# Softmax sums of batches 4 to 7: from TensorE matmuls with a matrix of ones to VectorE sums over turned 32 by 32 squares

## The chip, the core and the metric

One core of a Trainium2 chip runs the whole kernel. The metric is the device time of one execution in microseconds (us). The engines are named as in the profile: PE (TensorE matmul) and PEld (its weight loads), DVE (VectorE), ACT (ScalarE), POOL (GpSimd) and SP (SyncE, used here only to issue transfers).

## What is computed

Attention with projected keys and values (8 batches, 8 heads, 1024 tokens, head size 64; keys and values are projected from 1024 rows down to 64), then a two-layer network with a hard-swish between, on 8192 tokens of width 512 and an inner width of 2048:

```python
k_proj = einsum('ks,bhsd->bhkd', E, k)          # 64 projected keys
v_proj = einsum('ks,bhsd->bhkd', F, v)
scores = (q @ k_proj^T) / sqrt(64)
attn   = exp(scores - max)                      # the kernel leaves the max out
attn   = attn / (sum(attn, axis=-1) + 1e-9)     # <- the softmax sums in question
x      = (attn @ v_proj), heads side by side    # 8192 x 512
h      = x @ w_in                               # 8192 x 2048
out    = (h * clip(h + 3, 0, 6) / 6) @ w_out    # 8192 x 512
```

For one batch the softmax sums are 8 heads x 1024 tokens: each adds 64 numbers.

## The kernel before, in words

A block `b` of the main loop (from line 632) runs the network of batch `b` and, woven into it, the attention of batch `b+1` (`second`) and the key and value projection of batch `b+2` (`third`). A block has two halves `t` of 512 tokens. A half has 16 first groups (`first_group`, line 512: 16 matmuls into one `mm` tile, then `h_out`: Relu by ACT into `r`, a multiply by DVE into `g`) and four slots in which a second group of the half before runs (`second_group`, line 521: 64 matmuls into one `mm` tile, which ACT copies to `o_sb` and SP sends out). From block 2 on the slots stand after first groups 3, 7, 11 and 15; numbered through a block they are slots 0 to 7. The table `plan` (lines 638 to 651) says at which quarter of which slot a piece of attention work is put in. The order on every engine's queue is the order in which the program text calls the instructions; no scheduler moves them.

For blocks 3 to 6 (attention of batches 4 to 7) the plan before is: slot 0, scores and exps of head pairs `j` = 1, 2 and 3 (`j = 0` was done in slot 6 of the block before); slot 1, `all_sums`; slot 3, the projection of batch `b+2`; slot 4, values and products of `j = 0, 1`; slot 6, values and products of `j = 2, 3`, and the scores of `j = 0` of the next batch. Small pieces are put off into the list `later`, one of which is popped after each first group.

`exps` (line 241) writes `aT[j]`, the exponentials: on partitions 64 `t` + key, 2 x 2 x 256 elements for parity `r`, head `a` of the pair and tokens. `all_sums` (line 269) makes all 16 rows of sums of a batch with eight matmuls against the 0/1 matrix `halves`, into one `mm` tile; ACT takes Ln, and after the next first group `spread` (line 282) lets ACT take Exp of its negative (so the inverse), SP writes 16 rows of 512 to DRAM (`rows`) and reads them back eight times, each time one head's row spread over 64 partitions, into the four `rec` tiles: four of these reads on SP's queue, four on POOL's. `scaled` (line 264) multiplies the values' tiles by `rec` on DVE and writes `xT`, the network's input of the next block.

Buffers that matter: four `mm` and four `at` tiles (lines 61, 62) are taken in turn by every matmul group, so a group waits until the reader of the tile four back is done. `rec` has four, `o_sb` four, `r` four, `aT` five buffers. `turn` (line 217) puts the transposes of the next keys (`kT`) and queries (`qT`) on SP's queue after slot 3, and POOL starts the loads of another batch when `qT` has landed.

Of the kernel before, what the change touches and what calls it, by code (L numbers as in the profile page):

```python
# [8 lines left out]
f32 = mybir.dt.float32  # L9
bf16 = mybir.dt.bfloat16  # L10
AF = mybir.ActivationFunctionType
ALU = mybir.AluOpType
# [3 lines left out]
def kernel(  # L16
# [11 lines left out]
    nc = tc.nc  # L28
    B, H, S, D = q.shape
    KP = E.shape[0]  # L30
# [3 lines left out]
    P = 128  # L34
    SO = S // P
    KO = d_model // P
    FO = d_ff // P
    TOK = 512
    NB = S // TOK
# [13 lines left out]
    dram = ctx.enter_context(tc.tile_pool(name="dram", bufs=2, space=bass.MemoryType.DRAM))  # L53
    kqv_pool = ctx.enter_context(tc.tile_pool(name="kqv", bufs=2))
    qT_pool = ctx.enter_context(tc.tile_pool(name="qT", bufs=2))
    att = ctx.enter_context(tc.tile_pool(name="att", bufs=2))
# [9 lines left out]
    def pmm():  # L66
        return ps_mm.tile([P, TOK], f32, tag="mm", name="mm")
# [5 lines left out]
    def g_tile():  # L73
        return gpool.tile([P, FO, TOK], bf16, tag="g", name="g")
# [10 lines left out]
    halves = consts.tile([P, 2, 2, NB, KP // 8], bf16, name="halves")  # L85
# [52 lines left out]
    for i in range(SB):  # L138
        c = slice(i * FO // SB, (i + 1) * FO // SB)
# [20 lines left out]
    def q_transposed(b):  # L160

        t = qT_pool.tile([P, KO, 2, TOK], bf16, tag="qT", name="qT")
        nc.sync.dma_start_transpose(t.rearrange("p j a (m n) -> p (j a m) n", n=P),
                                    kqv[b]["q"].rearrange("p h s d -> p (h s d)"))
        return t
# [11 lines left out]
    def rec_tile():  # L177
        return att.tile([P, 2, TOK], f32, tag="rec", name="rec", bufs=4)
# [14 lines left out]
    class Attention:  # L193
# [47 lines left out]
        def exps(self, j, tiles, when=lambda f: f()):  # L241
            self.aT[j] = aT = att.tile([P, 2, 2, HT], bf16, tag="aT", name="aT", bufs=KO + 1)
            for r in range(2):
                when(lambda r=r: nc.scalar.activation(aT[:, r].rearrange("p a n -> p (a n)"), tiles[r],  # L244
                                                      AF.Exp, scale=scale))


        def quads(self, stationary, j, allocs):
            tiles = [alloc() for alloc in allocs]
            for t in range(NB):  # L250
                for a in range(2):
                    r, c = t * KP, a * D
                    nc.tensor.matmul(tiles[t][c:c + D].rearrange("p (r n) -> p r n", r=2),  # L253
                                     stationary(r, 2 * j + a),
                                     self.aT[j][r:r + KP, :, a, :], start=True, stop=True)
            return tiles

        def sums(self, j, *allocs):
# [10 lines left out]
        def all_sums(self):  # L269
            den = pmm()  # L270
            for i in range(2):
                for c in range(4):
                    j, a = 2 * i + c // 2, c % 2
                    nc.tensor.matmul(den[32 * c:32 * c + 32].rearrange("p (r n) -> p r n", r=2),  # L274
                                     halves[:, i].rearrange("p i t n -> p (i t n)"), self.aT[j][:, :, a, :],
                                     start=(i == 0), stop=(i == 1))
            few = att.tile([P, TOK], f32, tag="few", name="few", bufs=1)
            nc.scalar.activation(few, den, AF.Ln)
            later.append(lambda: self.spread(few))


        def spread(self, few):
            nc.scalar.activation(few, few, AF.Exp, scale=-1.0)
            rows = dram.tile([H * NB, TOK], f32, tag="rows", name="rows")
            nc.sync.dma_start(out=rows, in_=few[::8])
            by_head = rows.rearrange("(c i t) n -> i c (t n)", c=4, t=NB)
            self.recs = [rec_tile() for _ in range(KO)]
            for h in range(H):
                (nc.sync, nc.gpsimd)[h % 2].dma_start(out=self.recs[h // 2][h % 2 * D:(h % 2 + 1) * D].rearrange("d t n -> d (t n)"),  # L289
                                  in_=by_head[h // 4, h % 4:h % 4 + 1].to_broadcast([D, NB * TOK]))  # L290

# [218 lines left out]
    def first_group(xT, t, g, fo):  # L512
        h_ps = pmm()
        h_part(h_ps, xT, t, fo, range(KO))
        h_out(h_ps, g, fo)
# [5 lines left out]
    def second_group(b, t, g, c, copy=None):  # L521
        o_dst = out_rows(b, t, c)
        if (b, t, c) == (B - 1, NB - 1, SB - 1):

            most = d_model * 3 // 4
            for piece, copy, dma in ((slice(0, most), nc.vector.tensor_copy, nc.sync),
                                     (slice(most, d_model), nc.scalar.copy, nc.scalar)):
                n = piece.stop - piece.start
                o_ps = pmm()[:, :n]
                for fo in range(FO):  # L530
                    in_columns(o_ps, g[:, fo, c * P:(c + 1) * P], w_out_sb[:, fo, piece],
                               start=(fo == 0), stop=(fo == FO - 1))
                o_sb = opool.tile([P, d_model], f32, tag="o_sb", name="o_sb")[:, :n]
                copy(o_sb, o_ps)  # L534
                dma.dma_start(out=o_dst[:, piece], in_=o_sb)
            return
        o_ps = pmm()
        for fo in range(FO):
            in_columns(o_ps, g[:, fo, c * P:(c + 1) * P], w_out_sb[:, fo, :],
                       start=(fo == 0), stop=(fo == FO - 1))  # L540
            if fo % SB == SB - 1:
                yield
        o_sb = opool.tile([P, d_model], f32, tag="o_sb", name="o_sb")
        (copy or nc.scalar.copy)(o_sb, o_ps)  # L544
        nc.sync.dma_start(out=o_dst, in_=o_sb)

    def whole(gen):
        for _ in gen:
            pass

    def x_tile():
        return xpool.tile([P, KO, NB, TOK], bf16, tag="xT", name="xT")
# [43 lines left out]
    second = Attention(1)  # L596
    second.xT = x_next

    def pop():
        if later:  # L600
            later.pop(0)()

    rows = [second_group(0, 0, g[0], c) for c in range(SB)]
# [27 lines left out]
    second = Attention(2)  # L631
    for b in range(1, B):
        if b + 1 < B:
            x_next = second.xT = x_tile()
        third = Attention(b + 2) if b + 2 < B else None


        plan = {}
        two = (pmm, pmm), (pat, pat)
        if b == 1:  # L640
            plan = {4: (4, second.all_scores), 5: (3, second.all_sums), 6: (2, second.first_values),
                    7: (2, lambda: second.some_values((2, 3), ((pmm, pmm), (pmm, pat))))}
        elif b + 1 < B:
            plan = {3 + (b == 2): (2, third.projected) if third else None,
                    4 + (b == 2): (2, lambda: second.some_values((0, 1), two)),
                    6: (2, lambda: second.some_values((2, 3), two, third))}
            if b == 2:
                plan.update({0: (2, second.projected), 1: (4, second.all_scores), 2: (4, second.all_sums)})
            else:
                plan.update({0: (1, lambda: second.some_scores((1, 2, 3), ((pmm, pmm), (pat, pat), (pat, pat)))),  # L650
                             1: (4, second.all_sums)})


        slots = (0, 4, 10, 15) if b == 1 else (3, 7, 11, 15)
        for t in range(NB):
            g = g_tile()
            for fo in range(FO):
                if b < 3 and t == 0 and fo < 2:

                    if fo == 0:  # L660
                        TwoGroups(xT, t, g).parts((0, 1, 2), (3,))
                else:
                    first_group(xT, t, g, fo)
                pop()
                if b == 1 and t == 0 and fo == 5:
                    second.projected()
                if not behind or fo not in slots:
                    continue
                n = t * SB + slots.index(fo)
                if (b, n) == (1, 7):  # L670
                    second.first_products()
                when, act = plan.get(n) or (None, None)

                rows = second_group(*behind[0], n % SB,
                                    nc.vector.tensor_copy if second and act == second.all_scores else None)
                for quarter in range(1, SB + 1):
                    next(rows) if quarter < SB else whole(rows)
                    if quarter == when:
                        act()
            behind = [(b, t, g)]  # L680
        if b == 1:
            later.append(lambda: qT_dma.update({3: q_transposed(3)}))
        second, xT = third, x_next
# [32 lines left out]
```

The softmax here doesn't subtract the row's maximum and nothing guards it: scores larger than these inputs give would overflow.

## Time and profile before

| what | value |
|---|---|
| median of 6 runs | 506.4 us (505.79 to 508.25) |
| the profiled execution: its time / its span | 505.89 us / 503.7 us |
| PE busy | 495.8 us, 98% of the span |
| DVE busy / ACT busy / POOL busy | 245.4 / 244.6 / 51.5 us |
| matmuls of `all_sums` (line 274), all batches | 48 in six groups, 379 ns each, several at a time |
| ACT's Ln and Exp of the sums (lines 278, 283) | 6 x 602 ns and 6 x 622 ns |
| DVE's multiply of a first group (line 510) | 256 x 687 ns |
| reads `rec<-rows`, issue to landing | 3.4 / 7.6 / 11.1 us (least, median, most) |
| writes `rows<-few`, issue to landing | 1.8 / 2.5 / 5.2 us |

The span is the time from the first to the last instruction in the profiler's record; the execution's own time has some 2.2 us more around it. A share of busy time is a mean over the whole span. "The chain that ended last" is followed back from the last instruction, at each step to what released it. Matmuls of 32 columns overlap: the duration of one says less than the time a run of them takes.

### The profile page before, as it was taken

To read this page: it belongs to the slowest core of one execution; us is meant where nothing else is said; L and a number is where in the kernel's file an instruction comes from. 1 tells how busy PE (TensorE), PEld (TensorE's weight loads), DVE (VectorE), ACT (ScalarE), POOL (GpSimd) and SP (SyncE) were. 2 spreads that over 40 slices of the span, in tenths; PEclk is the share of its full clock that TensorE was granted. 3 is DMA by queue.
4 is the path that set the end of the run, shared out by engine and by line. 5 is a ranking of instruction groups with operands and counts; after the bars stand their busy time and mean duration, and the time that the engine had idled before them with its cause. 6 is when DMAs were issued, how large, how long until landed. Compare 5 with 4: busy or idle time off the path is not lost.

```text
span 503.7 us, 18691 instructions
## 1 busy us (share of the span) xinstructions
PE 495.8 (98%) x8562; PEld 245.8 (49%) x8562; DVE 245.4 (49%) x384; ACT 244.6 (49%) x425; POOL 51.5 (10%) x82
## 2 busy tenths in 40 slices
PE   7999999999999999999999999999999999999997
PEld 3554554444454444444454444554444444444444
DVE  3572736834753573436633654446552365334420
ACT  3757476655355445533564344652456444343431
POOL 8620020021020120012001020010000100000000
PEclk9999999999999999999999999999999999999999
DMA  9999979689839989379933799156111711101112
GB/s 169 198 205 207 187 144 232 148 139 232 224 62 220 269 160 210 79 210 166 212 77 89 169 173 216 45 152 178 44 44 46 189 47 44 43 26 42 45 44 87
DMA packets 78815, 68.91 MB, mean 137 GB/s; under 512 B 36400, under 2 KB 67376, under 8 KB 78736
## 3 DMA queue, kind: packets, MB, share of 16 engines
q0 software_dynamic: 34400, 35.66, 42.4%
q1 hardware_dynamic: 44112, 31.73, 22.4%
q8 instruction: 67, 1.10, 0.9%
q10 hardware_dynamic: 224, 0.33, 0.2%
q14 instruction: 12, 0.10, 0.1%
HBM read 71.83 MB, written 16.97 MB: 176 GB/s over the span
## 4 chain that ended last, share of the span: by engine, by line
PE 92%; DMA 6%; POOL 1%; issue 1%; ACT 0%; DVE 0%; POOLq 0%; ACTq 0%
PE mm L175 85%; PE at L175 2%; DMA w_in_sb<-in_moe_w_in_dram 2%; DMA rec<-rows 2%; DMA k<-in_k_dram 1%; DMA rows<-few 1%; PE mm L253 1%; PE at L235 1%; PE mm L235 1%; PE at L253 1%; PE mm L274 1%; PE at L421 0%; POOL q L109 0%; POOL k L113 0%; POOL rec L289 0%
## 5 line engine op out<-in xcount | busy, mean ns | idle before, releaser
L510 DVE SCALAR_TENSOR_TENSOR g<-r,mm 128x512 bf16<-128x512 f32 x256 | 174.4, 687 | 190.0 <-ACT r L509 189.2
L175 PE MATMUL mm<-w_out_sb,g 128*32 128x512 bf16 (+3 forms) x3904 | 235.9, 376 | 0.0
L175 PE MATMUL mm<-xT,w_in_sb 128*32 128x512 bf16 (+1 forms) x3840 | 231.3, 379 | 0.6 <-DVE xT L266 0.4
L509 ACT ACTIVATE r<-mm 128x512 f32<-128x512 f32 x256 | 153.1, 600 | 71.4 <-PE mm L175 67.9
L175 PEld LDWEIGHTS <-w_in_sb 128*32 128x32 bf16 (+1 forms) x3840 | 110.3, 98 | 111.1 <-issue 1.7
L175 PEld LDWEIGHTS <-g 128*32 128x32 bf16 (+1 forms) x3904 | 109.3, 98 | 111.5 <-issue 6.7
L544 ACT COPY o_sb<-mm 128x512 f32<-128x512 f32 x57 | 33.4, 587 | 146.5 <-PE mm L175 141.5
L289 POOL DMA_DIRECT2D rec<-rows x24 | 12.6, 531 | 191.9 <-DVE g L510 131.4
L244 ACT ACTIVATE aT<-at 128x512 bf16<-128x512 f32 x38 | 21.2, 626 | 7.6 <-PE at L235 7.6
L266 DVE TENSOR_TENSOR xT<-at,rec 128x512 bf16<-128x512 f32 x31 | 19.8, 681 | 5.8 <-ACT rec L187 5.8
L266 DVE TENSOR_TENSOR xT<-mm,rec 128x512 bf16<-128x512 f32 x25 | 16.0, 685 | 5.2 <-PE mm L253 4.9
L211 DVE CAST kp<-at 64x512 bf16<-64x512 f32 x14 | 9.0, 678 | 11.6 <-PE at L175 11.6
L244 ACT ACTIVATE aT<-mm 128x512 bf16<-128x512 f32 x18 | 9.6, 598 | 10.3 <-PE mm L235 10.3
L175 PE MATMUL at<-k,e_t 128*32 128x512 bf16 (+1 forms) x104 | 13.3, 379 | 0.0
L175 PE MATMUL at<-v,f_t 128*32 128x512 bf16 (+1 forms) x104 | 13.2, 379 | 0.0
L225 POOL COPY mark<-qT 1x1 bf16<-1x1 bf16 x5 | 0.9, 177 | 118.7 <-DMA qT<-q 118.7
L214 DVE CAST vp<-at 64x512 bf16<-64x512 f32 x14 | 9.7, 694 | 0.4
L175 PEld LDWEIGHTS <-e_t 128*32 128x32 bf16 (+1 forms) x104 | 5.8, 98 | 5.9
L534 DVE COPY o_sb<-mm 128x384 f32<-128x384 f32 x1 | 0.6, 558 | 15.2 <-DMA out_dram<-o_sb 15.2
L235 PEld LDWEIGHTS <-kT 64*64 64x64 bf16 x224 | 5.7, 106 | 4.3 <-issue 3.3
L96 PE MATMUL mm<-ones 128*128 128x512 bf16 x18 | 6.3, 471 | 1.5 <-DVE halves L86 1.5
L544 DVE COPY o_sb<-mm 128x512 f32<-128x512 f32 x6 | 4.1, 686 | 6.0 <-PE mm L175 6.0
(70 smaller groups left out, 149.2 us busy)
## 6 DMA issues: line engine op xcount, KB each, us to landing
out_dram<-o_sb SPq DMA_DIRECT2D x63, 256.0 KB, 3.5
k<-in_k_dram POOLq DMA_DIRECT2D x7, 1024.0 KB, 11.3
v<-in_v_dram POOLq DMA_DIRECT2D x7, 1024.0 KB, 16.6
q<-in_q_dram POOLq DMA_DIRECT2D x7, 1024.0 KB, 20.4
rec<-rows SPq DMA_DIRECT2D x24, 256.0 KB, 7.4
rec<-rows POOLq DMA_DIRECT2D x24, 256.0 KB, 7.6
w_out_sb<-in_moe_w_out_dram POOLq DMA_DIRECT2D x4, 512.0 KB, 16.0
w_in_sb<-in_moe_w_in_dram POOLq DMA_DIRECT2D x5, 256.0 KB, 9.6
```

The costliest lines, as they stand in the source:

```text
L96: nc.tensor.matmul(ps, ones[:, :P], ones, start=True, stop=True)
L175: nc.tensor.matmul(ps[lo:lo + width[0]], stationary[:, lo:lo + width[0]], moving, **flags)
L211: nc.vector.tensor_copy(self.kp[:, :, a, :], self.ps[:KP].rearrange("p (h d) -> p h d", d=D))
L214: nc.vector.tensor_copy(self.vp[a * KP:(a + 1) * KP], self.ps[KP:].rearrange("p (h d) -> p h d", d=D))
L235: nc.tensor.matmul(tiles[r][t * KP:(t + 1) * KP, a * HT:(a + 1) * HT], self.kT[r * D:(r + 1) * D, 2 * j + a, :], qT[r * D:(r + 1) * D, j, ...
L244: when(lambda r=r: nc.scalar.activation(aT[:, r].rearrange("p a n -> p (a n)"), tiles[r], AF.Exp, scale=scale))
L253: nc.tensor.matmul(tiles[t][c:c + D].rearrange("p (r n) -> p r n", r=2), stationary(r, 2 * j + a), self.aT[j][r:r + KP, :, a, :], start=Tr ...
L266: when(lambda t=t: nc.vector.tensor_mul(self.xT[:, j, t, :], av[t], rec[:, t]))
L289: (nc.sync, nc.gpsimd)[h % 2].dma_start(out=self.recs[h // 2][h % 2 * D:(h % 2 + 1) * D].rearrange("d t n -> d (t n)"), in_=by_head[h // 4 ...
L509: nc.scalar.activation(r, h_ps, AF.Relu, bias=0.5, scale=1.0 / 6.0)
L510: nc.vector.scalar_tensor_tensor(g[:, fo, :], r, 1.0, h_ps, op0=ALU.min, op1=ALU.mult)
L544: (copy or nc.scalar.copy)(o_sb, o_ps)
```

## The change

The sums of batches 4 to 7 are made by DVE. `add_up(j)` sums `aT[j]` over squares of 32 partitions by 32 tokens that are turned on the way (`apply_transpose`), one instruction for each `j`: 128 x 1024 bf16 in, 128 x 32 f32 out. `spread_sums` turns the collected 128 x 128 sums again, adds the two halves of 32 keys (a copy to bring them to the same partitions, then an add, for each `t`), inverts 64 x 128 numbers, writes them to DRAM with two transfers in pieces of 32 numbers, and reads them back eight times, all on SP's queue. So that 32 neighbouring tokens lie beside each other, `exps` stores `aT` with head before parity, and the matmuls that read it (`quads`, `all_sums`) take 512 neighbouring elements. That layout holds for batches 1 to 7. Batches 2 and 3 keep `all_sums` and `spread`. In blocks 3 to 6 the plan becomes: slot 0, scores and exps as before, then `add_up(0)`; slot 1 at its half, `add_up(1, 2)`; slot 2 at its half, `add_up(3)` and `spread_sums`; slot 3, projection as before; slot 5 (before: 4), values and products of `j = 0, 1`; slot 6 as before.

```diff
         def exps(self, j, tiles, when=lambda f: f()):
             self.aT[j] = aT = att.tile([P, 2, 2, HT], bf16, tag="aT", name="aT", bufs=KO + 1)
             for r in range(2):
-                when(lambda r=r: nc.scalar.activation(aT[:, r].rearrange("p a n -> p (a n)"), tiles[r],
+                when(lambda r=r: nc.scalar.activation(aT[:, :, r, :], tiles[r].rearrange("p (a n) -> p a n", a=2),
                                                       AF.Exp, scale=scale))
+
+        def weights(self, j, a):
+            return self.aT[j][:, a].rearrange("p r n -> p (r n)")
...
-                    nc.tensor.matmul(tiles[t][c:c + D].rearrange("p (r n) -> p r n", r=2),
-                                     stationary(r, 2 * j + a),
-                                     self.aT[j][r:r + KP, :, a, :], start=True, stop=True)
+                    nc.tensor.matmul(tiles[t][c:c + D], stationary(r, 2 * j + a),
+                                     self.weights(j, a)[r:r + KP], start=True, stop=True)
...
+        def add_up(self, *js):
+            if 0 in js:
+                self.parts = att.tile([P, KO, 32], f32, tag="parts", name="parts", bufs=1)
+            for j in js:
+                nc.vector.tensor_reduce(out=self.parts[:, j], op=ALU.add, axis=mybir.AxisListType.X, apply_transpose=True,
+                                        in_=self.aT[j].rearrange("p a r n -> p (a r n)").rearrange(
+                                            "p (c i) -> p c i", i=32))
+
+        def spread_sums(self):
+            turned, other = [att.tile([P, KO * 32], f32, tag="turned", name="turned", bufs=2) for _ in range(2)]
+            inv = att.tile([KP, KO * 32], f32, tag="inv", name="inv", bufs=1)
+            nc.vector.transpose(turned, self.parts.rearrange("p j c -> p (j c)"))
+            for t in range(NB):
+                here, there = slice(t * KP, t * KP + 32), slice(t * KP + 32, (t + 1) * KP)
+                nc.vector.tensor_copy(other[here], turned[there])
+                nc.vector.tensor_add(inv[t * 32:(t + 1) * 32], turned[here], other[here])
+            nc.vector.reciprocal(inv, inv)
+            rows = dram.tile([NB, KO, 32, 32], f32, tag="turned_rows", name="turned_rows")
+            for t in range(NB):
+                nc.sync.dma_start(out=rows[t].rearrange("j c i -> c j i"),
+                                  in_=inv[t * 32:(t + 1) * 32].rearrange("c (j i) -> c j i", j=KO))
+            by_head = rows.rearrange("t j (a c) i -> j a t (c i)", a=2)
+            self.recs = [rec_tile() for _ in range(KO)]
+            for j in range(KO):
+                for a in range(2):
+                    nc.sync.dma_start(out=self.recs[j][a * D:(a + 1) * D],
+                                      in_=by_head[j, a:a + 1].to_broadcast([D, NB, TOK]))
...
         elif b + 1 < B:
-            plan = {3 + (b == 2): (2, third.projected) if third else None,
-                    4 + (b == 2): (2, lambda: second.some_values((0, 1), two)),
+            plan = {5: (2, lambda: second.some_values((0, 1), two)),
                     6: (2, lambda: second.some_values((2, 3), two, third))}
+            if third:
+                plan[4 if b == 2 else 3] = 2, third.projected
...
             else:
-                plan.update({0: (1, lambda: second.some_scores((1, 2, 3), ((pmm, pmm), (pat, pat), (pat, pat)))),
-                             1: (4, second.all_sums)})
+                def last_sums():
+                    second.add_up(3)
+                    second.spread_sums()
+
+                def three_scores():
+                    second.some_scores((1, 2, 3), ((pmm, pmm), (pat, pat), (pat, pat)))
+                    second.add_up(0)
+
+                plan.update({0: (1, three_scores), 1: (2, lambda: second.add_up(1, 2)), 2: (2, last_sums)})
```

## The prediction

> **What bounds the kernel now.** I read the page's busy table, then the chain that ended last in order of time, then the table of stretches, one per block, then the timelines of DVE and SP around the sums of batch 4 (block 3).
>
> ```profile
> PE 495.8 (98%) x8562; PEld 245.8 (49%) x8562; DVE 245.4 (49%) x384; ACT 244.6 (49%) x425; POOL 51.5 (10%) x82
> ```
> ```profile
> 198.66 9.61 PE mm L175 x176
> 208.27 0.43 PE mm L274 x8
> 208.71 12.09 PE mm L175 x224
> 220.79 1.73 PE at L175 x32
> 222.52 6.91 PE mm L175 x128
> 229.43 0.34 PE mm L253 x4
> ...
> 243.91 0.34 PE mm L253 x4
> 244.25 0.22 PE at L253 x4
> 244.47 0.22 PE at L235 x8
> ```
> ```profile
> 208.30:268.15 59.85, 59.85 (x1116) 29.29 (x1112) 29.54 (x44) 28.87 (x50) 4.96 (x8) 1.00 0.69 146
> ```
>
> The chain (start, length, what) is unbroken PE from 131 to 500 us. The stretch (length, then busy time of PE, PEld, DVE, ACT, POOL, then PE's granted clock) says so too: in a block of 59.85 us PE is busy for all of it at full clock, DVE and ACT for half. So a matmul taken out there is worth its place in the chain, and work given to DVE costs only what makes PE wait. PE runs 224 matmuls in 12.09 us, 54.0 ns each: a first group (16) is 0.86 us, a second group (64) 3.45 us. The eight of the sums take 0.43 us, the same rate.
>
> ```profile
> 205.50 0.69 DVE L510 SCALAR_TENSOR_TENSOR g<-r,mm 128x512 bf16<-128x512 f32 x1 [0.18 <-ACT r L509]
> 210.25 0.69 DVE L510 SCALAR_TENSOR_TENSOR g<-r,mm 128x512 bf16<-128x512 f32 x1 [4.06 <-ACT r L509]
> 211.26 1.41 DVE L510 SCALAR_TENSOR_TENSOR g<-r,mm 128x512 bf16<-128x512 f32 x2 [0.32 <-ACT r L509]
> 212.84 0.69 DVE L510 SCALAR_TENSOR_TENSOR g<-r,mm 128x512 bf16<-128x512 f32 x1 [0.17 <-ACT r L509]
> 217.16 0.69 DVE L510 SCALAR_TENSOR_TENSOR g<-r,mm 128x512 bf16<-128x512 f32 x1 [3.63 <-ACT r L509]
> ```
>
> DVE has a hole of some 4 us in every slot, while the second group runs (in brackets: its idle time). The new DVE work goes into these holes, behind the last multiply of the four first groups.
>
> **Removed from PE.** In each of four blocks 8 matmuls: 0.43 us each time, 1.73 us in all. Both neighbours have the same 128x32 form, so no gap goes or comes with them. ACT loses Ln and Exp, 1.22 us a block, off the path; one `mm` tile a block is no longer taken.
>
> **Added to DVE.** No row shows a turned sum, so I price it from rows with one input.
>
> ```profile
> L374 DVE CAST kp<-at 64x128 bf16<-64x128 f32 x8 | 1.9, 278 | 2.4 <-PE at L371 2.4
> L534 DVE COPY o_sb<-mm 128x384 f32<-128x384 f32 x1 | 0.6, 558 | 15.2 <-DMA out_dram<-o_sb 15.2
> L405 DVE COPY rec<-at 128x1024 bf16<-128x1024 bf16 x2 | 1.4, 683 | 0.0
> ```
>
> From 278 ns at 128 elements to 558 at 384 is 1.09 ns an element and 138 ns fixed: 1024 elements are 1.26 us. Least is the 683 ns of L405's 1024 elements; as most I take the element time twice, once to fill and once to empty the turned square: 2.38 us. I take 1.26. The rest of `spread_sums` is a turn, two copies and two adds of 128 elements, 0.28 us each by L374, and a reciprocal of 128 elements, 0.28 or, at eight times the elements' part, 1.26 us: 1.7 us, at most 2.7. A block gets 4 x 1.26 + 1.7 = 6.7 us, so DVE rises from 29.5 to 36 us of 59.4.
>
> Does it fit? Slot 0: `aT[0]` is old, DVE is free from 198.40 (last multiply at 197.71) to 202.91; even 2.38 fits. Slot 1: two sums from 206.19 end at 208.7. Without the sums' matmuls the first groups 8 to 11 run from 208.27 to 211.72. A multiply after a slot starts 1.54 us after the second group's end (215.62 to 217.16), so the next is due at 209.81. It fits with 1.1 us left. PE itself waits only if the multiply of group 8 isn't done (0.69) when slot 2's second group wants its `mm` tile at 211.72: the limit for one sum is (211.72 - 0.69 - 206.19) / 2 = 2.42 us. Slot 2: DVE is free 1.37 us after group 11 (220.44 - 219.07 for group 15), at 213.09; 1.26 + 1.7 end at 216.05, next due 216.72; PE waits from 217.94 on (slot 3's tile, 215.18 + 3.45 - 0.69). With both highest prices the end is 218.2, a wait of 0.2 us.
>
> The Trainium skill, page "VectorE: DVE Perf Modes", section "Rules for kernel authors", speaks against the change: of `tensor_reduce` on a hot path it says "Expect 1× — it's the slowest DVE op. Consider restructuring". Its section on the 1x mode makes the sum one element a cycle, an estimate of (1024 + 150) / 0.96 = 1.22 us, which fits the same hole; the page's warning would count only if DVE were the hot path, and the block's row says it is not.
>
> **Moved and added transfers.** The inverse is ready at 216.1 instead of 210.7. On SP there now stand two writes of 32 KB and eight reads; before, one write, four reads, and four on POOL.
>
> ```profile
> 210.76 0.51 SPq L285 DMA_DIRECT2D rows<-few  x1
> 213.69 2.75 SPq L289 DMA_DIRECT2D rec<-rows  x4
> 216.53 8.71 SPq L545 DMA_DIRECT2D out_dram<-o_sb  x2
> 225.41 1.25 SPq L218 DMA_TRANSPOSE kT<-kp  x1
> 226.71 4.29 SPq L163 DMA_TRANSPOSE qT<-q  x1
> ```
>
> Issues take 0.51 us each: the second write goes at 216.6, lands 2.5 (at most 5.2) us later, 219.1 to 221.8. Eight reads at 2.75 / 4 = 0.69 us are issued by 224.6 to 227.3, the four for `j = 0, 1` by 221.9 to 224.6; with 7.4 (at most 11.1) us to landing these are in by 229 to 236, the others by 232 to 238. Values now stand in slot 5: 229.43 - 0.43 + 6.91 = 235.9, products from 236.6. So the later slot pays for the later sums: 7 us of margin at the medians, none to speak of at the worst; `j = 2, 3` are wanted at 243.5 and have 6 us. A product that waited for `rec` would hold DVE's queue, hence the multiplies of slot 5's groups and, past some 1.7 us (0.5 free behind the four products, 1.2 of the `mm` tiles as in slot 1), PE.
>
> Behind the eight reads on SP wait the outputs of slots 2 and 3 (four `o_sb` buffers: not wanted for two slots), then `kT` and `qT`. The program reuses a DMA semaphore after eight transfers, so `qT` also waits for the fourth read to land, 229 to 236. With 6.1 us from issue to landing (8.3 at most in the trace) it comes at 235 to 244; the scores of the next batch want it at 244.0 (244.47 - 0.43). POOL's loads behind it started at 233.4 before, start 2 us later and have until 280. POOL loses four issues, 2.1 us a block.
>
> The Trainium skill, page "DMA: Bandwidth & Descriptors", section "Specifications", asks for pieces of at least 512 B; below, a transfer does a read-modify-write. The new write goes in pieces of 128 B, 256 of them, where the old one had 16 of 2 KB. No run here shows that price; 7 us more would still only use up the margin.
>
> **Layout.** `exps` writes two runs of 256 elements instead of 512, the matmuls read one run instead of two. L274 reads two runs at 54 ns like all others, so nothing is to be gained; for ACT the worst is two instructions of 256 (378 ns each in this trace) for one of 600, 0.9 us over the six in slot 0. ACT is idle 0.3 us behind them and the `mm` tiles give 1.2 us (211.72 - 0.69 - 209.81) more: nothing.
>
> **Sum.** -4 x 0.432 = -1.73 us. The profiled execution would go from 505.89 (span 503.7) to 504.16. It lies 0.5 us below the median of the runs, 506.4; the median would be 504.7, -0.34%. About 0.3%, 1.5 us, is what this kernel's measurement can tell from no change, so the whole gain lies just past that.
>
> **Rivals.**
> 1. The turned sum is slow, the one that ends slower. It decides from 2.42 us on (slot 1): each us more in one sum costs 2 us of PE there and, from about 3 us on, 1 us in slot 2. The gain of 0.43 is gone at 2.64 us. At four times the element time, 4.6 us, slot 1 loses 2 x (4.6 - 2.42) = 4.4 and slot 2 some 2.5: 27 us in four blocks, 531. For it: no turned sum in the trace. Against: no one-input row of DVE's above 1.1 ns an element.
> 2. The spread comes late (small pieces, one queue): `rec` past 238.3 or `qT` past 244.0 stalls PE by the same amount, four blocks (three for `qT`). 2 us late in each costs 6 to 8 us less 1.7: 510 to 513. For it: the worst landings use up the margin. Against: the medians leave 7 us.
> 3. Nothing measurable: part of the 1.73 is lost in small waits (a multiply late by tenths, other gaps at changes of matmul form, 0.12 us at the first values), 505.2 to 506.4. For it: the gain is thin. Against: PE has no idle time left for the loss to hide in.
>
> **How the numbers follow.** Forecast 0.67, rival 1 0.09, rival 2 0.08, rival 3 0.16. The forecast's own range is 503.8 to 505.4 (run noise of half a us; one less transition gap). The forecast falls short of 0.3% by noise in some 0.06 of cases, and rival 3 ends slower in 0.03: faster 0.61, same 0.19, slower 0.20. The range for 8 in 10 takes in rival 3 and its edge: 503.7 to 506.8.
>
> **What would show it.** Right: 32 fewer matmuls; block stretches of 59.4 us with PE busy throughout; `parts` near 1.26 us; products in slot 5 waiting for PE, not for a DMA; `mark` for `qT` near 235. Wrong: PE waiting for the multiplies into `g` in slots 2 or 3 (rival 1), for `xT` or `qT` in slots 5 or 6 (rival 2). What makes the prediction wrong is a turned sum above 2.4 us or a spread that takes over 20 us.

## The result, and the profile after

| | before | after |
|---|---|---|
| median | 506.53 us (505.64 to 508.88, 44 runs) | 503.75 us (503.07 to 507.24, 19 runs) |
| ratio, 95% interval | | 0.9946 [0.9936, 0.9956] |
| profiled execution / its span | 505.89 / 503.7 us | 503.87 / 502.1 us |
| PE / DVE / ACT / POOL busy | 495.8 / 245.4 / 244.6 / 51.5 us | 495.4 / 272.8 / 240.7 / 43.0 us |

The change makes the kernel faster by 2.7 us (0.54%); 1.73 us were forecast. PE's busy time falls by only 0.4 us in this pair, because in the first 20 us it is 1.0 us higher (17.25 against 16.22 us); what the change is worth is read from the blocks. First the chain that ended last in the kernel after (start, length, what), block 3 and the start of block 4:

```profile
199.08 21.70 PE mm L175 x400
220.78 1.73 PE at L175 x32
222.51 13.81 PE mm L175 x256
236.32 0.34 PE mm L256 x4
...
243.90 0.34 PE mm L256 x4
244.24 0.22 PE at L256 x4
244.45 0.22 PE at L235 x8
```

The piece `L274 x8` is gone and the 176 and 224 matmuls beside it have become one run of 400, still at 54 ns each. The values of `j = 0, 1` (now line 256) stand one slot later. From block 3 on there is no wait in it. The same stretch, from one projection to the next, in the kernel before and then in the kernel after (length, then busy time of PE, PEld, DVE, ACT, POOL with counts, granted clock, DMA share, GB/s):

```profile
220.79:280.65 59.86, 59.86 (x1117) 29.39 (x1112) 29.54 (x44) 28.86 (x50) 4.95 (x8) 1.00 0.72 151
```
```profile
220.78:280.21 59.43, 59.43 (x1109) 29.00 (x1104) 36.38 (x54) 27.93 (x48) 2.80 (x4) 1.00 0.73 147
```

Eight matmuls fewer, 0.43 us less, PE busy for all of both; DVE has 6.8 us more to do and nobody waits for it. The DVE timeline of the kernel after shows how near that is:

```profile
206.53 2.37 DVE L299 TRANSPOSE_TENSOR_REDUCE parts<-aT 128x32 f32<-128x1024 bf16 x2
210.24 0.69 DVE L543 SCALAR_TENSOR_TENSOR g<-r,mm 128x512 bf16<-128x512 f32 x1 [1.35 <-ACT r L542]
...
213.43 1.24 DVE L299 TRANSPOSE_TENSOR_REDUCE parts<-aT 128x32 f32<-128x1024 bf16 x1
...
216.17 0.94 DVE L313 RECIPROCAL inv<-inv 64x128 f32<-64x128 f32 x1
217.15 0.69 DVE L543 SCALAR_TENSOR_TENSOR g<-r,mm 128x512 bf16<-128x512 f32 x1
```

In slot 1 DVE is idle for 1.35 us behind the two sums. In slot 2 the reciprocal ends just as group 12's multiply is due (no brackets: no idle time before it). DVE's groups by form, for the prices (busy time, mean ns):

```profile
L299 DVE TRANSPOSE_TENSOR_REDUCE parts<-aT 128x32 f32<-128x1024 bf16 x16 | 19.4, 1229 | 0.0
L313 DVE RECIPROCAL inv<-inv 64x128 f32<-64x128 f32 x4 | 3.8, 945 | 0.1
L312 DVE TENSOR_TENSOR inv<-turned 32x128 f32<-32x128 f32 x8 | 2.2, 280 | 0.3
L311 DVE COPY turned<-turned 32x128 f32<-32x128 f32 x8 | 1.8, 219 | 0.2
L308 DVE STREAM_TRANSPOSE turned<-parts 128x128 f32<-128x128 f32 x4 | 1.2, 312 | 0.1
```

So four blocks account for 1.73 us of the 2.7. The last microsecond is not in the blocks. The end of the program: the last run of matmuls and the DMA table of the stretch behind it, before and then after:

```profile
422.32 77.88 PE mm L175 x1504
q8 instruction: 1, 0.02, 1.5%
issues: line engine op xcount, KB each, median us to landing
out_dram<-o_sb SPq DMA_DIRECT2D x1, 192.0 KB, 2.5
out_dram<-o_sb ACTq DMA_DIRECT2D x1, 64.0 KB, 2.1
```
```profile
421.02 77.88 PE mm L175 x1504
issues: line engine op xcount, KB each, median us to landing
out_dram<-o_sb SPq DMA_DIRECT2D x1, 192.0 KB, 1.9
out_dram<-o_sb ACTq DMA_DIRECT2D x1, 64.0 KB, 1.6
```

Before, one load on the instruction queue (`q8`, 16 KB) falls among the last two output transfers and both land later; after, there is none there. From PE's last matmul (500.20 and 498.90) to the end of the span it is 3.5 us before and 3.2 us after. And the time outside the span is 1.79 us in the mean of 19 runs, where the kernel before has 2.12 (29 runs). These two, the end and the time outside, were the open question for the experiments.

### The profile page after: what moved, and what is told of

The parts are those of the page before. It is cut to its first block, busy times and chain, and to the rows that moved or that the text cites. A ratio compares the mean times of both kernels' runs of the same rounds, so it can differ in the third digit from the quotient of the medians.

```text
span 502.1 us, 18625 instructions
## 1 busy us (share of the span) xinstructions
PE 495.4 (99%) x8530; PEld 245.7 (49%) x8530; DVE 272.8 (54%) x424; ACT 240.7 (48%) x417; POOL 43.0 (9%) x66
## 4 chain that ended last, share of the span: by engine, by line
PE 93%; DMA 4%; POOL 1%; issue 1%; ACT 1%; DVE 0%; POOLq 0%; ACTq 0%
PE mm L175 86%; PE at L175 2%; DMA rec<-rows 2%; DMA k<-in_k_dram 1%; DMA rows<-few 1%; PE mm L256 1%; PE at L235 1%; PE mm L235 1%; PE at L256 1%; PE at L454 1%; PE at L420 0%; POOL q L109 0%; PE at L434 0%; PE mm L454 0%; POOL k L113 0%
## 5 line engine op out<-in xcount | busy, mean ns | idle before, releaser
L299 DVE TRANSPOSE_TENSOR_REDUCE parts<-aT 128x32 f32<-128x1024 bf16 x16 | 19.4, 1229 | 0.0
L96 PE MATMUL mm<-ones 128*128 128x512 bf16 x18 | 7.4, 549 | 1.5 <-DVE halves L86 1.5
## 6 DMA issues: line engine op xcount, KB each, us to landing
v<-in_v_dram POOLq DMA_DIRECT2D x7, 1024.0 KB, 16.4
```

Source lines behind the costliest of these rows:

```text
L96: nc.tensor.matmul(ps, ones[:, :P], ones, start=True, stop=True)
L299: nc.vector.tensor_reduce(out=self.parts[:, j], op=ALU.add, axis=mybir.AxisListType.X, apply_transpose=True, in_=self.aT[j].rearrange("p a ...
```

## The experiments

**Is it POOL's queue?** One run gives POOL half of the reads back, the other takes them away from the kernel before.

```diff
-                    nc.sync.dma_start(out=self.recs[j][a * D:(a + 1) * D],
+                    (nc.sync, nc.gpsimd)[a].dma_start(out=self.recs[j][a * D:(a + 1) * D],
```

> The changed kernel with every second of the eight reads of a batch on POOL's queue again, as before the change. The chain of PE in blocks 3 to 6 stays as it is (59.43 us a block). Theory A (the part of the gain beyond the 1.73 us of the removed matmuls, about 1.0 us, comes from the 16 reads that left POOL's queue, at the end of the program and outside the span): the time goes back by 0.7 to 1.0 us, to a ratio near 0.9965, and the time outside the span rises from 1.77 to about 2.2 us. Rival B (the queue has nothing to do with it): ratio stays near 0.9946, 1.77 us outside the span.

Measured: 503.55 us, ratio 0.9943 [0.9925, 0.9962], 1.78 us outside the span, 59.43 us a block. Theory A falls: 16 reads more on POOL cost nothing.

```diff
-                (nc.sync, nc.gpsimd)[h % 2].dma_start(...
+                (nc.sync, nc.gpsimd)[h % 2 if self.b < 4 else 0].dma_start(...
```

> The kernel before, with all eight reads of batches 4 to 7 on SP's queue, POOL's none. PE's blocks stay at 59.86 us unless a product waits for its reads (slot 4 wants them some 16 us after the write). Theory A: faster by 0.7 to 1.0 us (ratio near 0.998), time outside the span 1.8 us in place of 2.2. Rival B: ratio 1.000 within 0.0007.

Measured: 506.56 us, ratio 0.9998 [0.9986, 1.0010]. That is rival B for the whole time. Yet the time outside the span did fall to 1.80 us, though in the run before it stayed at 1.78 with POOL's reads back. So the reads on POOL don't set it either.

**Do the matmuls carry the gain?** The eight matmuls run again in blocks 3 to 6; nobody reads their result, the sums still come from DVE.

```diff
+                def idle_sums():
+                    den = pmm()
+                    for i in range(2):
+                        for c in range(4):
+                            nc.tensor.matmul(den[32 * c:32 * c + 32], halves[:, i].rearrange("p i t n -> p (i t n)"),
+                                             second.weights(2 * i + c // 2, c % 2), start=(i == 0), stop=(i == 1))
...
+                def two_sums():
+                    second.add_up(1, 2)
+                    later.append(idle_sums)
...
```

> The changed kernel with the eight matmuls against the 0/1 matrix run again in blocks 3 to 6, their result unread. Theory of the forecast (PE's removed matmuls are 0.432 us a block): block stretches of 59.86 us and 1.73 us more than the changed kernel, a ratio near 0.998. Rival (the gain comes from elsewhere, the matmuls fill places that were free): within 0.3 us of the changed kernel, ratio 0.9946 to 0.9955.

Measured: 506.28 us, ratio 1.0005 [0.9987, 1.0022]. Its chain and its stretch from projection to projection:

```profile
198.41 10.47 PE mm L175 x192
208.89 0.43 PE mm L696 x8
209.32 11.22 PE mm L175 x208
```
```profile
220.54:280.40 59.86, 59.86 (x1117) 29.36 (x1112) 36.41 (x54) 27.95 (x48) 2.81 (x4) 1.00 0.75 146
```

DVE does the whole new work (36.4 us), and the block is back at 59.86. So the matmuls' place in PE's order is the gain of the blocks and the DVE work is free: the theory is right. But it predicted a return of 1.73 us, and by the medians 2.5 came back (the ratio's interval is 0.9 us to either side). The kernel's DMA table at the end shows the load again:

```profile
q8 instruction: 1, 0.02, 1.7%
issues: line engine op xcount, KB each, median us to landing
out_dram<-o_sb SPq DMA_DIRECT2D x1, 192.0 KB, 2.9
out_dram<-o_sb ACTq DMA_DIRECT2D x1, 64.0 KB, 2.4
```

**Is it the layout?** The kernel before with the new order of `aT` alone (`exps` and the operands of `quads` and `all_sums` as in the diff of the change).

```diff
-                when(lambda r=r: nc.scalar.activation(aT[:, r].rearrange("p a n -> p (a n)"), tiles[r],
+                when(lambda r=r: nc.scalar.activation(aT[:, :, r, :], tiles[r].rearrange("p (a n) -> p a n", a=2),
```

> The kernel before with only the new layout of the exponentials (two runs of 256 written, one run of 512 read by the matmuls). Forecast: nothing, ratio 1.000 within 0.0007, values' matmuls 0.34 + 0.22 us as before, ACT's exps within 0.03 us of 0.60 to 0.63. Rival C (the layout brings the rest of the gain): faster by about 1 us, ratio 0.998.

Measured: 506.54 us, ratio 1.0000 [0.9988, 1.0011]. ACT's exps take 598 and 629 ns in the mean, as before (598 and 626). Rival C falls; the layout is worth nothing, as forecast.

**Is it where the instruction loads fall?** PE's list before is 2 x 8562 instructions and the page counts 67 loads of together 1.10 MB: one load of 16 KB for 256 instructions, that is for 128 pairs of weight load and matmul, 6.9 us at 54 ns. In the trace of the kernel before the ten loads from 432.4 to 494.4 us stand 6.9 us apart. The removed sums are 64 instructions, a quarter of a period. Four runs shift the phase by small pairs (28 ns each) in place of warm-up matmuls at the start:

```diff
-    busy(12)
+    busy(8)
+
+    ps = pmm()
+    for _ in range(36):
+        nc.tensor.matmul(ps[:32, :32], ones[:, :32], ones[:, :32], start=True, stop=True)
```

The second has `busy(4)` and 72, the third and the fourth `busy(1)` and 107.

> The changed kernel with 32 small pairs of weight load and matmul more on PE, put at the start in place of four of the warm-up matmuls: PE's instruction list is as long as before the change (64 more), the work of the main loop is the changed kernel's. Theory P (phase: the instruction queue loads 16 KB, 256 of PE's instructions, every 6.9 us, and with 64 instructions more one load falls on the last two output transfers, as it does before the change and not after it): 0.6 to 1.0 us above the changed kernel, near 504.5 (ratio 0.9963), landing of the last transfers 2.5 and 2.1 us in place of 1.9 and 1.6, block stretches still 59.43 us. Rival Q (the list's length has nothing to do with it, the removed matmuls simply are worth more than 1.73 us): within 0.3 us of 503.7.

> As the run before with 64 small pairs (128 instructions more). Theory P: the load at the end comes 1.7 us earlier again, at about the last matmul's end, and touches the output transfers less: between 503.7 and 504.5. Rival Q: 503.7.

> As the run before with 96 small pairs (192 instructions more). Theory P: the load falls 1.9 us before the last matmul's end and is over before the last transfers; the time is the changed kernel's again, 503.7 within 0.3. A third theory L (a longer list costs in itself) would give more than with 32 or 64 pairs, above 504.5.

> The kernel before with 96 small pairs at the start in place of eleven warm-up matmuls: its list is 192 instructions longer, 256 more than the changed kernel's, so the loads fall as in the changed kernel. Theory P: 0.6 to 1.0 us faster than the kernel before (ratio 0.998 to 0.9988) with no work taken out. Rival Q: ratio 1.000; theory L: slower.

| run | median, us | ratio to before | last landings, us | end of PE to end of span, us |
|---|---|---|---|---|
| after + 64 instructions | 504.56 (6 runs) | 0.9953 [0.9939, 0.9967] | 2.9, 2.5 | 4.1 |
| after + 128 | 504.38 (5) | 0.9943 [0.9929, 0.9956] | 2.2, 1.7 | 3.3 |
| after + 192 | 504.65 (6) | 0.9955 [0.9941, 0.9969] | 1.9, 1.6 | 3.2 |
| before + 192 | 506.32 (12) | 0.9987 [0.9975, 1.0000] | 1.9, 1.6 | 2.9 |

The kernel before stood at 506.90 in these runs. Where the loads fall, theory P is right in all four: the load comes back to the end with 64 instructions more and leaves it with 192, in the kernel before too. The profiles (all but the one at half rate, further below) sort by the last load's start against the end of PE's last matmul:

- from 0.0 to 0.3 us behind it (before, the reads on SP, the matmuls put back, the layout, 64 instructions more): landings of 2.5 to 3.0 us and 2.1 to 2.5, a tail of 3.5 to 4.1 us, mean 3.8;
- some 0.5 us ahead of it (128 more): 2.2 and 1.7 us, a tail of 3.3;
- over 2 us ahead (after, the reads on POOL, the two with 192 more, and three of the runs below): 1.9 and 1.6 us, a tail of 2.9 to 3.2, mean 3.1.

Between the first and the last that is 0.7 us. In the medians the size isn't shown. By the ratios the first run is 0.35 us above the changed kernel and the fourth 0.65 us below the kernel before: theory P's way, the first by less than its 0.6 us. But the third, which should have been the changed kernel's again, is 0.45 us above it, and the intervals overlap. At 504.65 us it even meets theory L (above 504.5); the fourth, faster with the longest list of all, speaks against L. The exchanged warm-up work changes the start as well, which these runs don't separate: block 3's projection begins at 221.25, 221.34, 220.43 and 224.19 us in the four profiles, at 220.78 in the changed kernel's and 220.79 in that of the kernel before.

**How much room has DVE?** The two sums of slot 1 made three times over.

```diff
-... 1: (2, lambda: second.add_up(1, 2)), ...
+... 1: (2, lambda: second.add_up(1, 2, 1, 2, 1, 2)), ...
```

> The changed kernel with the two sums of slot 1 made three times over (six instead of two; the same values are written again). By the limit of the prediction's slot 1 (PE waits when the multiply of group 8 is not done as slot 2's second group starts, 4.85 us of DVE's work in that hole): six sums at 1.19 us are 7.1 us, so PE waits some 2.3 to 2.6 us in slot 2 of each of four blocks, block stretches of 61.9 us, 513 to 514 us. Rival (the `mm` tiles give less or more room than reckoned): no wait at all (503.8), or one of over 4 us a block (above 520).

Measured once: 511.78 us. Its chain, and what PE waited for (us in total, times, longest):

```profile
206.27 6.79 DVE parts L299 x6
213.06 0.58 DVE g L543
213.64 0.04 issue
213.68 8.82 PE mm L175 x160
```
```profile
PE mm L175 <- DVE g L543: 7.5, 4, 1.9
```

The six sums enter the chain, and PE waits 1.9 us in each block for a multiply into `g`. Six sums take 6.87 us on DVE's timeline, so the room is 6.87 - 1.9 = 5.0 us against 4.85 reckoned. The limit is there, and it is the one of the prediction. The time is below the 513 to 514 us expected: in a row of six a sum took 1.14 us, not 1.19, and the room is 0.15 us larger.

**Was the later slot needed?** Values of `j = 0, 1` back in slot 4.

```diff
-            plan = {5: (2, lambda: second.some_values((0, 1), two)),
+            plan = {(5 if b == 2 else 4): (2, lambda: second.some_values((0, 1), two)),
```

> The changed kernel with the values of j = 0, 1 back in slot 4 of blocks 3 to 6. Theory (the later slot pays for the later sums): the products would want `rec` at 229.8 in block 3's frame, the first four reads are issued by 222.2 and land 6.6 us (at most 10.6) later, 228.8 to 232.8: DVE waits for the reads there, 0 to 3 us, and PE for 0 to 1.5 us a block: 503.8 to 510. Rival (the reads are in time for slot 4 also, the move is worth nothing): products wait for PE only, 503.7.

Measured: 503.76 us, ratio 0.9946 [0.9930, 0.9961], which is the changed kernel's. DVE's timeline there:

```profile
229.03 0.70 DVE L214 CAST vp<-at 64x512 bf16<-64x512 f32 x1
229.76 1.29 DVE L268 TENSOR_TENSOR xT<-mm,rec 128x512 bf16<-128x512 f32 x2
230.96 1.28 DVE L268 TENSOR_TENSOR xT<-at,rec 128x512 bf16<-128x512 f32 x2
```

The products follow at once and don't wait for the reads. My theory falls: the move of the values is worth nothing at these landings.

**Can it go further?** Batch 3's sums (block 2) on DVE too, its reads on POOL.

```diff
-                plan.update({0: (2, second.projected), 1: (4, second.all_scores), 2: (4, second.all_sums)})
+                plan.update({0: (2, second.projected), 1: (4, second.all_scores),
+                             2: (1, lambda: second.add_up(0, 3, 1)), 3: (1, batch_3_sums)})
...
```

> The changed kernel with batch 3's sums (block 2) on DVE too: three sums in slot 2, the fourth and the spreading in slot 3, its eight reads on POOL's queue so that the transposes on SP's are not held up. Forecast: eight matmuls less, 0.43 us, 503.3 (ratio 0.9938) if the reads land before slot 5's products (first four issued by 229, in by 236, wanted at 236.7 in block 3's frame). Rival (the spread is late, block 2 has the loads of another batch beside it): PE waits 1 to 4 us in slot 5, 504 to 508.

> The kernel that also makes batch 3's sums on DVE, looked at once more, since the profiled execution before ran its matmuls at half rate from the first to the last (117 ns each) and tells nothing of the timed ones (510 to 515 us at granted clocks of 0.990 to 0.993). Theory: PE stalls 2 to 4 us in slots 5 or 6 of block 2, waiting for `xT` (late `rec`) or for the transposes, and after the stall the granted clock is halved for two or three stretches of 3.4 us, which cost 1.7 us each. Rival: no stall in block 2; the time is lost elsewhere (slots 2 and 3, DVE late with the multiplies).

Measured in the first: 1047.89 us in the profiled execution, 512.28 us in the median of the other five, ratio 1.0119 [1.0091, 1.0147]. In the second: 512.45 us, one execution. The forecast of 503.3 fails, and its rival's 504 to 508 is passed too. What PE waited for in the second, the chain there, and its stretches around the wait:

```profile
PE at L235 <- DMA qT<-q: 7.2, 1, 7.2
```
```profile
173.09 17.96 DMA qT<-q
191.04 0.04 issue
191.08 0.64 PE at L235 x6
191.73 15.47 PE mm L175 x240
```
```profile
182.00:185.40 3.40, 1.91 (x36) 0.57 (x24) 2.11 (x4) 0.27 (x1) 0.00 (x0) 1.00 1.14 105
185.40:188.80 3.40, 0.00 (x0) 0.10 (x1) 0.69 (x2) 0.00 (x0) 0.00 (x0) 0.64 1.33 121
188.80:192.20 3.40, 1.12 (x16) 0.47 (x19) 0.60 (x2) 0.43 (x1) 0.69 (x2) 0.50 0.84 222
192.20:195.60 3.40, 3.40 (x40) 1.29 (x36) 0.00 (x0) 0.94 (x3) 2.15 (x3) 0.50 0.61 77
195.60:199.00 3.40, 3.40 (x60) 1.48 (x56) 1.30 (x2) 1.87 (x4) 0.00 (x0) 0.86 1.12 149
```

The spread, one slot later, lies on top of the transposes: its reads were issued from 169.37 to 174.19, `qT` at 173.09. `qT` took 18 us to land (median in the changed kernel 9.6), and slot 6's scores waited 7.2 us for it. That the reads beside it made `qT` late is argued from this overlap; no run separates it from the loads of another batch. DVE waited for reads too (3.1 us in slot 6). Meanwhile the granted clock (third figure from the end) falls to 0.5 and is full again only from 199 on: the next 240 matmuls took 15.5 us in place of 13.1, 2.4 us more. 7.2 + 2.4 is more than twenty times the 0.43 us to be gained. The expectation of the second run named both the wait and the lower clock; the wait is longer than its 2 to 4 us. No version tried here beats the changed kernel.

## Why the prediction was right, and where it fell short

- *The range*: 503.75 us lies at the very edge of the 503.7 to 506.8 forecast, and just below the narrower 503.8 to 505.4. The mechanism forecast was right; that the time still fell within the wide range is partly luck, since another microsecond came from two terms that the sum didn't have (below).
- *Removed from PE, 1.73 us*: 0.43 us in each of four blocks, shown by the profile and by putting the matmuls back. Right.
- *Added to DVE*: 1.23 us for a turned sum against 1.26, a price borrowed from other instructions, where anything up to 2.42 would have done; 2.4 us with the gaps for the rest of the spreading against 1.7 (at most 2.7). The reciprocal is the dear one, 0.945 us within its 0.28 to 1.26. DVE's share of a block is 36.4 us, as reckoned. The work in slot 2 should have ended 0.7 us before group 12's multiply was due and ends just at it; by the prediction's limit 1.2 us more were free before PE would wait. Rival 1 is out.
- *The rule on* `tensor_reduce` *in the Trainium skill* (page "VectorE: DVE Perf Modes", section "Rules for kernel authors"): its warning did not bear, since DVE had holes. The price estimated from that page, 1.22 us, agrees with 1.229.
- *Transfers*: the two writes are 16 KB each (not 32, as I had it); in pieces of 128 B they landed in 1.4 to 1.9 us, faster than the old ones (1.8 to 5.2). The rule of the Trainium skill's page "DMA: Bandwidth & Descriptors", section "Specifications", on pieces under 512 B shows no price in these landings. It isn't a clean test, since the new writes are half as large and go out at another time. The reads were in before slot 4 would have wanted them: "so the later slot pays for the later sums" failed as a need. `qT` came later than I had it (POOL's `mark` at 239.1 against 235, some 0.4 of it this execution's start) and kept 5 us of margin. Rival 2 is out for blocks 3 to 6; a late `qT` is what sank batch 3's sums.
- *The sum*: it failed by being confined to the blocks. "The profiled execution would go from 505.89 (span 503.7) to 504.16": it went to 503.87, 2.7 us by the ratio. Missing are the end of the program, 0.7 us between profiles with and without an instruction load among the last outputs (0.3 in this pair), and 0.33 us outside the span; 1.73 + 0.7 + 0.33 = 2.76. In the profiled pair itself it is 1.73 + 0.3 + 0.4, less 0.4 for a later start of block 3. The first of the two extra terms has its place and its later landings shown in the rows, its size in the medians not. The cause of the second stays open: the kernel before and its variants with the new layout and with 192 instructions more have 2.1 us, all the others 1.8, and neither POOL's reads nor PE's list sorts them so.
- *Rival 3* rested on "the whole gain lies just past" what can be told; with the two extra terms it was well past.

## What to carry to other kernels

Where one engine runs without a gap, count what leaves its queue and look for holes of other engines in the timeline, at the place, not in the shares: 6.8 us of DVE work a block was free because it came in pieces under 5 us behind the last multiply of a slot. The same move one slot later, in a block with the loads of another batch beside it, cost twenty times its gain through one late transfer. And a change of some tenths of a percent must be read to the program's very end: where the last instruction load falls made 0.7 us between the tails, beside 1.73 us for the edit itself.

## What the runs showed that I had not expected

The length of PE's instruction list, counted modulo 256, moves the last load against the last outputs: 0.7 us of tail between the profiles. The Trainium skill, page "Runtime: NRT & Kernel Launch", section "Instruction fetch mechanics", states refills in blocks of 16 KiB, 256 instructions, their cost "mostly hidden". The 16.4 KB a load here (1.10 MB in 67) agree. At the last outputs the load wasn't hidden: they landed 0.5 to 1.1 us later beside it.

In the one trace where PE waited 7 us, the granted clock stood at 0.5 for some 10 us, from within the wait on (the stretches above: 3.4 x (0.36 + 0.5 + 0.5 + 0.14) / 0.5, if the clock was either 0.5 or full), which added 2.4 us to the next 240 matmuls.
